# Attention and a two-product SiLU network on one core: the products' instructions rank 100 places earlier in the scheduler

## The chip, the cores and the metric

The kernel runs on one core of one Trainium2 chip. The metric is the device time of one execution in microseconds (us); several runs are taken and their median is given. A core has TensorE (PE; its weight loads are listed apart as PEld), VectorE (DVE), ScalarE (ACT), GpSimd (POOL) and SyncE (SP), which here only issues DMAs. Each engine works through its own list of instructions in order and waits on semaphores for the others.

## The reference

Attention with a second, linear memory read, over 8 batches and 8 heads of 576 tokens and 64 features, all in float32; then a network without bias on the 4608 x 512 result. The inputs q, k, v, M_prev, z_prev and beta belong to the first part, the two weights to the second (they arrive as 64-bit floats).

```python
scores = scale * np.matmul(q, k.transpose(0, 1, 3, 2))
scores = np.where(causal, -1000000000.0, scores)
a = np.exp(scores - scores.max(-1, keepdims=True))
a /= a.sum(-1, keepdims=True) + 1e-09
local = np.matmul(a, v)
q_p = phi(q)                                   # where(x > 0, x, exp(x) - 1) + 1
mem_out = einsum('bhsd,bhde->bhse', q_p, M_prev) / (einsum('bhsd,bhd->bhs', q_p, z_prev)[..., None] + 1e-06)
attn = g * mem_out + (1 - g) * local           # g = sigmoid(beta), one per head
x = attn.transpose(0, 2, 1, 3).reshape(B * S, H * D)
h = x @ w_in                                   # 4608 x 512 by 512 x 2048
out = (h * (1.0 / (1.0 + np.exp(-h)))) @ w_out # 4608 x 2048 by 2048 x 512
```

## The kernel before

**Two streams and a third.** Attention (`attention`, with `scores` and `values` for each head) goes over the 64 heads, the eight heads of a batch in a row. The products (`ffn`) go over 18 units of 256 tokens. A unit can begin when all eight heads of the last batch that it touches are done: units 0 and 1 need 8 heads, 2 and 3 need 16, 4 and 5 need 24, 6 to 8 need 32, 9 and 10 need 40, 11 and 12 need 48, 13 and 14 need 56, the rest 64. The third stream (`preparation`) turns the 32 pieces of the weights into a high and a low float32r part; twelve of the pieces are written to a scratch in memory and streamed from there again for each unit (`flow`), the others stay in place.

**A head.** `scores` transposes q and k on DVE (line 221), splits them into a high and a low part (lines 230 to 237; the first ten heads are left whole and multiplied in float32), makes four score tiles and two halves of the fifth (matmuls of lines 250, 271 and 274), each with a masked minimum on DVE (252, 284) and an exponential on ACT (254, 294), scales them on POOL (304) and works out the memory read's features (lines 325 to 334). `values` transposes features and probabilities on TensorE (351, 376, 384, 393), copies them out in two parts (lines 358, 359, 406, 407), multiplies them by M_prev and v (414, 422) and writes half a head at a time into the tile `xt` of its two heads (line 430, for the first ten heads line 425).

**A unit.** `split_x` copies and splits the tokens (lines 504 and 505: four tiles `xu` out of six buffers). Then come eight steps p: 24 matmuls of 256 columns into `h` (line 552), which has one PSUM bank, and every second time one of two others once all heads are traced; the 12 matmuls of 512 columns of the step before into the two accumulators `acc` (line 532); then tanh on ACT (563), the product with h on DVE (564, which gives the bank of h free), and the two parts of `g` on POOL (567) and DVE (568). At p = 6 the next unit's split is traced if its heads are done. At the end `acc` goes out (578).

**What sets the order.** The streams are Python generators. The loop at line 589 takes one step of attention at a time, some preparation, and as many steps of the products as the rates 0.20 (first two units) and 0.22 (later) allow: 17 steps make a unit, and ten steps of attention a head. What is left of the products when attention's generator ends is traced after the loop. The order of tracing is an instruction's place. It isn't yet the order of the engines' lists: the tile framework simulates the program in time and gives each engine, whenever it comes free, the instruction with the lowest place among those whose data and buffers are there. So an engine may take work from far later in the program if nothing earlier is ready. SP's list of DMAs, on which all loads stand (attention's two heads ahead, the streamed weights when one of two buffers comes free), is made in the same way.

Of the kernel before, what the change touches and what calls it, by code (L numbers as in the profile page):

```python
# [33 lines left out]
FFN_RATE = 0.22  # L34
FIRST_RATE = 0.2
FIRST_UNITS = 2
W_EARLY = 2


@with_exitstack  # L40
def memory_attention_then_silu_ffn(ctx, tc, q, k, v, M_prev, z_prev, beta, w_in, w_out, out):
# [132 lines left out]
    def load_next(n):  # L174
        if n < len(order):
            with tc.issue_after(anchor["sp"]) if "sp" in anchor else ExitStack():
                loaded.append(load_weight(*order[n]))

    def preparation():
        for n, x in enumerate(order):  # L180
            with tc.issue_after(anchor["dve"]):
                split_weight(*x, loaded.pop(0))
            load_next(n + W_AHEAD)
            ready.add(x)
            yield
# [13 lines left out]
    def load_rest(b, h):  # L199
        qn = qrest[(b * H + h) % 2]  # L200
        nc.sync.dma_start(out=qn[:, 0:NQ - 1], in_=q[b, h, 0:(NQ - 1) * P].rearrange("(c p) d -> p c d", p=P))
        nc.sync.dma_start(out=qn[0:LAST, NQ - 1], in_=q[b, h, S - LAST:S])
        vr = pool.tile([P, NQ, D], F32, tag="vr", name="vr", bufs=3)
        nc.sync.dma_start(out=vr[:, 0:NQ - 1], in_=v[b, h, 0:(NQ - 1) * P].rearrange("(c p) d -> p c d", p=P))
        for p0 in (0, LAST):
            nc.sync.dma_start(out=vr[p0:p0 + LAST, NQ - 1], in_=v[b, h, (NQ - 1) * P:S])
        mr = pool.tile([P, D], F32, tag="mr", name="mr", bufs=NB["mr"])
        for p0 in (0, 64):
            nc.sync.dma_start(out=mr[p0:p0 + 64], in_=M_prev[b, h])
        zb = pool.tile([P, D], F32, tag="zb", name="zb", bufs=NB["zb"])  # L210
        anchor["sp"] = nc.sync.dma_start(out=zb, in_=z_prev[b, h:h + 1].to_broadcast([P, D])).ins
        return qn, vr, mr, zb
# [223 lines left out]
    def attention():  # L436
        todo = [(b, h) for b in range(B) for h in range(H)]
        raws, rests = [], []
        for n in range(2):
            raws.append(load_raw(*todo[n]))  # L440
            if n == 0:
                load_next(0)
            rests.append(load_rest(*todo[n]))
            if n == 0 and W_EARLY > 1:
                load_next(1)
        for n in range(W_EARLY, W_AHEAD):
            load_next(n)
        second = iter(())
        for n in range(len(todo) + 1):

            first, made = iter(()), {}
            if n < len(todo):
                first = scores(*todo[n], raws.pop(0), rests.pop(0), made, n < N_WHOLE)
            one = two = True
            m = 0
            while one or two:
                for _ in range(FIRST_STEPS):
                    one = one and next(first, "end") != "end"
                if two and next(second, "end") == "end":
                    two = False  # L460
                    done[0] = n
                if m == 2 and n + 2 < len(todo):
                    raws.append(load_raw(*todo[n + 2]))
                m += 1
                yield
            if n < len(todo):
                b, h = todo[n]
                if n + 2 < len(todo):
                    rests.append(load_rest(*todo[n + 2]))
                if h % 2 == 0:  # L470
                    xt[b, h // 2] = pool.tile([P, S], F32, tag=f"xt{h // 2}", name="xt", bufs=2)
                second = values(b, h, made, xt[b, h // 2], n < N_WHOLE)
# [113 lines left out]
    att, prep, prod = attention(), preparation(), ffn()  # L586
    steps, produced, steps_made = 0, 0.0, 0
    going = True
    while going:
        going = next(att, "end") != "end"  # L590
        steps += 1
        started = done[0] >= H
        while going and len(ready) < min(2 * KF, steps * (PREP_AFTER if started else PREP_RATE) / A_STEPS):
            next(prep)
        if started:
            produced += (FFN_RATE if steps_made >= FIRST_UNITS * F_STEPS else FIRST_RATE) * F_STEPS / A_STEPS
        while going and produced >= 1.0:
            said = next(prod, "end")
            if said == "wait":
                produced = min(produced, 1.0)  # L600
                break
            if said == "prepare":
                next(prep)
                continue
            produced -= 1.0
            steps_made += 1
# [28 lines left out]
```

## Time and profile before

| what | value |
|---|---|
| median of 3 runs | 1333.85 us (1330.49 to 1334.98) |
| the profiled execution: its own time | 1331.87 us |
| its span, first to last instruction | 1330.1 us |
| mean granted TensorE clock | 0.978 |
| TensorE busy: matmuls, weight loads | 1269.9 us (95%), 1084.7 us (82%) |
| DVE, ACT, POOL busy | 963.4, 805.2, 798.1 us |
| DMA | 190.39 MB, 143 GB/s, 50.8% of 16 engines' span |

A row of the page or of a view by line names the line of the kernel, the engine, the operation, and what is written from what by the program's names. Rows in order of time begin with the start and the duration in us, and show in brackets how long the engine sat idle before and who ended that. Rows by stretch give the stretch, its length, and then the busy time of each engine with the number of instructions; behind them stand the granted clock, the DMA engines' share and GB/s. The ends of matmuls are modelled, so neighbouring matmuls overlap in the rows.

### The profile page before, as it was taken

The numbers are of one execution on the slowest core, as the hardware profiler recorded it, in microseconds if no ns is written. First come the engines' busy times: TensorE is split into PE (matmuls) and PEld (weight loads), VectorE is DVE, ScalarE is ACT, GpSimd is POOL, SyncE is SP. The second block draws the span as 40 slices with busy tenths as digits, with TensorE's granted clock in tenths as the row PEclk, the third lists the DMA queues.
The fourth block names the chain that finished last, engine by engine and source line by source line (L and its number), as shares of the span: only waits on it lengthen the run. The fifth ranks groups of instructions, "written<-read, shape, count | busy, mean of one in ns | idle before, by whom it ended". The sixth has DMA issues, their size and how long they took to land.

```text
span 1330.1 us, 24649 instructions
## 1 busy us (share of the span) xinstructions
PE 1269.9 (95%) x7858; PEld 1084.7 (82%) x7858; DVE 963.4 (72%) x2580; ACT 805.2 (61%) x1999; POOL 798.1 (60%) x1169
## 2 busy tenths in 40 slices
PE   6988989999999999999999999999999999999998
PEld 2343458898989899899989898989898889899997
DVE  7988985788888878877888787778878875322222
ACT  6777765667676767667776676666767663111111
POOL 6888994676666667766677665656576653101110
PEclk9986799999999999999999999999999999999999
DMA  6766555554555545555555455455545432444444
GB/s 163 191 177 176 151 152 159 136 140 134 135 150 137 151 116 135 152 137 151 136 149 140 136 139 136 131 149 136 137 134 145 128 101 80 155 137 155 156 159 143
DMA packets 302994, 190.39 MB, mean 143 GB/s; under 512 B 258832, under 2 KB 267024, under 8 KB 302864
## 3 DMA queue, kind: packets, MB, share of 16 engines
q1 hardware_dynamic: 302864, 188.82, 50.8%
q8 instruction: 62, 1.02, 0.3%
q14 instruction: 68, 0.56, 0.1%
HBM read 173.02 MB, written 15.73 MB: 142 GB/s over the span
## 4 chain that ended last, share of the span: by engine, by line
PE 71%; DVE 13%; ACT 6%; DMA 4%; issue 3%; POOL 2%; SPq 1%; DVEq 0%; POOLq 0%; ACTq 0%
PE h L552 27%; PE acc L532 24%; PE x L422 7%; PE s L250 5%; PE tp L376 4%; DVE s L252 2%; PE x L414 1%; PE tq L351 1%; DMA zb<-in_z_prev 1%; DVE xu L505 1%; DMA flow<-wo_s 1%; DVE th L564 1%; DVE wy L152 1%; DVE wy L159 1%; ACT p L254 1%
## 5 line engine op out<-in xcount | busy, mean ns | idle before, releaser
L552 PE MATMUL h<-xu,wi 128*128 128x256 f32 x2592 | 373.8, 287 | 10.0 <-DVE th L564 7.3
L552 PEld LDWEIGHTS h<-xu,wi 128*128 128x128 f32 x2592 | 342.6, 191 | 24.9 <-DVE th L564 5.9
L304 POOL TENSOR_SCALAR p<-p,st 128x384 f32<-128x384 f32 (+3 forms) x320 | 186.1, 600 | 127.4 <-DVE st L302 121.2
L532 PE MATMUL acc<-wo,g 128*128 128x512 f32 x864 | 244.8, 399 | 0.0
L567 POOL TENSOR_SCALAR g<-th 128x512 fp32r<-128x512 f32 x144 | 90.9, 631 | 236.8 <-DVE th L564 205.7
L532 PE MATMUL acc<-flow,g 128*128 128x512 f32 x864 | 230.9, 395 | 0.7 <-DMA flow<-wo_s 0.7
L254 ACT ACTIVATE p<-s,st 128x128 f32<-128x128 f32 (+3 forms) x256 | 134.9, 528 | 123.2 <-DVE st L252 93.7
L564 DVE SCALAR_TENSOR_TENSOR th<-th,h 128x512 f32<-128x512 f32 x144 | 98.5, 685 | 130.5 <-ACT th L563 128.0
L532 PEld LDWEIGHTS acc<-flow,g 128*128 128x128 f32 x864 | 158.9, 188 | 33.9 <-DMA flow<-wo_s 1.8
L532 PEld LDWEIGHTS acc<-wo,g 128*128 128x128 f32 x864 | 150.0, 189 | 20.1 <-POOL p L304 0.5
L563 ACT ACTIVATE th<-h 128x512 f32<-128x512 f32 x144 | 85.6, 595 | 128.1 <-PE h L552 127.3
L407 DVE TENSOR_TENSOR pl<-tp,ph 128x384 fp32r<-128x384 f32 x216 | 118.4, 550 | 38.1 <-ACT ph L406 33.9
L568 DVE TENSOR_TENSOR g<-th,g 128x512 fp32r<-128x512 f32 x144 | 104.8, 728 | 50.5 <-POOL g L567 49.3
L252 DVE CUSTOM_DVE_ANT_0 s<-s,mask 128x128 f32<-128x128 f32 (+3 forms) x256 | 125.4, 492 | 11.5 <-PE s L250 6.7
L376 PE MATMUL tp<-ident,p 128*128 128x128 f32 x640 | 123.0, 292 | 8.5 <-DVE qp L359 3.7
L552 PE MATMUL h<-xu,flow 128*128 128x256 f32 x864 | 126.7, 284 | 0.0
L406 ACT CAST ph<-tp 128x384 fp32r<-128x384 f32 x216 | 104.7, 490 | 23.6 <-PE x L422 14.7
L552 PEld LDWEIGHTS h<-xu,flow 128*128 128x128 f32 x864 | 114.1, 190 | 0.9 <-issue 0.3
L376 PEld LDWEIGHTS tp<-ident,p 128*128 128x128 f32 x640 | 81.5, 147 | 37.4 <-POOL p L304 9.3
L235 POOL TENSOR_TENSOR ql<-tt,qq 64x512 fp32r<-64x512 f32 x54 | 73.2, 1356 | 20.6 <-ACT qq L231 11.3
L328 POOL TENSOR_TENSOR r<-e,zb 128x320 f32<-128x320 f32 x64 | 59.8, 935 | 42.4 <-DVE e L327 35.4
L422 PE MATMUL x<-pl,vs 128*128 128x256 f32 x324 | 81.7, 307 | 0.0
(103 smaller groups left out, 2430.2 us busy)
## 6 DMA issues: line engine op xcount, KB each, us to landing
flow<-wo_s SPq DMA_DIRECT2D x144, 512.0 KB, 3.5
flow<-wi_s SPq DMA_DIRECT2D x72, 512.0 KB, 3.8
raw<-in_k SPq DMA_DIRECT2D x128, 72.0 KB, 2.3
raw<-in_q SPq DMA_DIRECT2D x128, 72.0 KB, 2.5
out<-o SPq DMA_DIRECT2D x36, 256.0 KB, 4.2
wraw<-in_moe_w_in SPq DMA_DIRECT2D x16, 512.0 KB, 4.4
qn<-in_q SPq DMA_DIRECT2D x64, 128.0 KB, 2.9
vr<-in_v SPq DMA_DIRECT2D x64, 128.0 KB, 2.6
```

Source lines behind the costliest of these rows:

```text
L252: anchor["dve"] = nc.vector.tensor_tensor_reduce(s, s, mask[:, 3 * P - P * i:], QS, 3.0e38, ALU.add, ALU.min, st[:, i:i + 1]).ins
L254: nc.scalar.activation(pt, s, AF.Exp, bias=st[:, i:i + 1], scale=-1.0, accum_out=st[:, 10 + i:11 + i])
L304: nc.gpsimd.tensor_scalar(pb[x], pb[x], st[:, 15 + x:16 + x], 1.0, op0=ALU.mult, op1=ALU.mult)
L376: nc.tensor.transpose(t[:, o:o + P], pb[i][:, P * j:P * j + P], ident)
L406: nc.scalar.copy(ph[:, 0:o], t[:, 0:o])
L407: nc.vector.tensor_tensor(out=pl[:, 0:cut], in0=t[:, 0:cut], in1=f(ph[:, 0:cut]), op=ALU.subtract)
L422: nc.tensor.matmul(x[0:rows, q0:n], vs[0:n_k, j], part[0:n_k, o:o + n - q0], start=False, stop=last)
L532: nc.tensor.matmul(acc[t], ta, tb, start=p == 0 and c == 0 and n == 0, stop=p == NP - 1 and c == 1 and n == len(terms) - 1)
L552: nc.tensor.matmul(h[:, c], ta, tb, start=kk == 0 and n == 0, stop=kk == KD - 1 and n == len(terms) - 1)
L564: nc.vector.scalar_tensor_tensor(out=th, in0=th, scalar=1.0, in1=h, op0=ALU.add, op1=ALU.mult)
L567: nc.gpsimd.tensor_scalar(hi, th, 1.0, 1.0, op0=ALU.mult, op1=ALU.mult)
L568: nc.vector.tensor_tensor(out=lo, in0=th, in1=f(hi), op=ALU.subtract)
```

## The change

The call that advances the products' generator by one step is put into a context that sets the place counter back by 100 for the instructions traced in it and restores it on leaving. Matmuls, vector work, the splits and the loads of streamed weights that are traced inside the loop all get these places. The products' steps traced after the loop, preparation and attention keep theirs. Nothing is computed in another way.

```diff
+AHEAD = 100
 ...
         while going and produced >= 1.0:
-            said = next(prod, "end")
+            with tc.high_priority(AHEAD):
+                said = next(prod, "end")
             if said == "wait":
                 produced = min(produced, 1.0)
                 break
```

## The prediction

> **What bounds the kernel now.** I read the page's shares and slices first, then the busy time by stretch, then the waits, then the order of time at the places where a unit of the products begins.
>
> ```profile
> PE 1269.9 (95%) x7858; PEld 1084.7 (82%) x7858; DVE 963.4 (72%) x2580; ACT 805.2 (61%) x1999; POOL 798.1 (60%) x1169
> PE   6988989999999999999999999999999999999998
> PEclk9986799999999999999999999999999999999999
> ...
> 0.00:180.00 180.00, 148.99 (x428) 67.39 (x428) 152.88 (x359) 132.92 (x316) 151.51 (x156) 0.86 0.63 168
> 180.00:1050.00 870.00, 848.42 (x5667) 769.62 (x5667) 698.61 (x1977) 595.41 (x1506) 582.95 (x909) 1.00 0.52 140
> 1050.00:1331.00 281.00, 272.47 (x1766) 247.70 (x1764) 111.89 (x246) 76.83 (x178) 63.65 (x106) 1.00 0.41 135
> ```
>
> The first rows are the page; the last three give length and then busy PE, PEld, DVE, ACT and POOL in a stretch. TensorE is the bound. Of its 60 us of idle time, 31.0 lie before 180 us (180 - 148.99), where attention runs without the products: the first unit of 256 tokens needs all heads of the first batch, so the change has nothing to put there. From 180 to 1050 us, where both run, 21.6 us are idle (870 - 848.42). That is the most that a better order can win there. The last stretch has 8.5 (281 - 272.47), drain at the end included.
>
> ```profile
> 250.00:1050.00 800.00, 779.90 (x5243) 713.14 (x5241) 649.06 (x1845) 553.28 (x1396) 538.18 (x845) 1.00 0.51 139
> ...
> 250.00:1050.00 800.00, 319.72 (x2218) 290.39 (x2218) 1.00 0.51 139
> 1140.00:1320.00 180.00, 100.70 (x765) 99.30 (x766) 1.00 0.46 153
> ...
> 250.00:1050.00 800.00, 42.39 (x94) 1.00 0.51 139
> ```
>
> All engines; then line 552's matmuls in the shared stretch and in the tail; then line 430's DVE additions, two a head. A unit has 192 matmuls of line 552. In the tail, where nothing else runs, 765 of them in 180 us are 3.98 units, **45.2 us of TensorE a unit**. In the shared stretch 2218 are 11.55 units and 94 halves are 47 heads: 17.0 us a head, 4.07 heads a unit. Of 779.9 us, 11.55 x 45.2 = 522 are the products', so a head takes (779.9 - 522) / 47 = **5.5 us of TensorE**. The rest of a head's 17.0 us is the products' filling.
>
> **The change, part by part.** No instruction is added or removed. The scheduler gives each engine, in simulated time, the ready instruction with the lowest place. Entering the context sets the place back by 100 and leaving restores it, so products traced in the loop rank 100 places earlier against attention. Those traced after the loop are not moved.
>
> How much is 100 places? One late head traces 41 matmuls and transposes, 27 DVE, 20 ACT and 16 POOL instructions and 12 DMAs (counted in the code): 116, so 0.86 head. If the releases of its some 40 tiles take places too, 0.64. I take 0.75 head. A unit's 17 steps at 0.22 x 17 / 9 a step are traced over 4.09 heads, so a head's place of products is 45.2 / 4.09 = 11.05 us of TensorE. TensorE is full, so what the products gain attention loses: x / 11.05 + x / 5.5 = 0.75 gives x = 2.75 us. The products come 2.75 us sooner; attention falls behind by 2.75 / 5.5 = 0.5 head, 8.5 us. **The shift between them is 11.3 us** (12.9 at 0.86, 9.6 at 0.64).
>
> *What is saved: waits of the h buffer.* It has one bank until attention is over.
>
> ```profile
> PE h L552 <- DVE th L564: 4.6, 8, 1.2
> PE h L552 <- DVE th L564: 7.3, 11, 1.6
> ...
> 797.13 0.28 PE L250 MATMUL s<-kk,ql 128*128 128x256 f32 x1
> 798.60 2.77 PE L552 MATMUL h<-xu,wi 128*128 128x256 f32 x21 [1.19 <-DVE th L564]
> ...
> 796.15 0.42 DVE L505 TENSOR_TENSOR xu<-xt,xu 128x256 fp32r<-128x256 f32 x1
> 796.49 0.82 DVE L290 TENSOR_TENSOR st<-st 64x1 f32<-64x1 f32 x1
> 797.24 0.41 DVE L505 TENSOR_TENSOR xu<-xt,xu 128x256 fp32r<-128x256 f32 x1
> 797.68 0.15 DVE L291 COPY st<-st 64x1 f32<-64x1 f32 x1
> 797.86 0.69 DVE L564 SCALAR_TENSOR_TENSOR th<-th,h 128x512 f32<-128x512 f32 x1
> ```
>
> The wait rows (total us, times, longest) are of 250 to 1050 us and of the whole span; below them stands one of these waits, with DVE's order ahead of it. Attention's L290 and L291 stand before th there (0.82 + 0.15 us) and would stand behind it. I take -4.6 us, between 0 (the splits, themselves products, delay th too) and -7.3.
>
> In a sentence by itself: the Trainium skill, Perfetto Trace Analysis, Optimization Strategy, says that a gap which repeats on the engine that should be full can mean too few buffers for the next tile. The eight waits fit it, since one bank is released late each time; by that rule a new order would leave them, and the sum below would be 4.6 us higher.
>
> *What is lost: tokens not yet there.* Units 2, 4 and 6 are the first to read a new batch, and their last split waits for that batch's eighth head.
>
> ```profile
> 314.64 0.49 DVE L505 TENSOR_TENSOR xu<-xt,xu 128x64 fp32r<-128x64 f32 x2
> 323.18 1.54 PE L532 MATMUL acc<-flow,g 128*128 128x512 f32 x6
> ...
> 450.70 0.42 DVE L430 TENSOR_TENSOR xt<-x,xb 64x256 f32<-64x256 f32 x1
> 453.20 1.04 DVE L505 TENSOR_TENSOR xu<-xt,xu 128x256 fp32r<-128x256 f32 x2
> 456.36 1.54 PE L532 MATMUL acc<-flow,g 128*128 128x512 f32 x6
> ...
> 589.88 1.33 DVE L505 TENSOR_TENSOR xu<-xt,xu 128x192 fp32r<-128x192 f32 x5 [1.62 <-ACT xu L504]
> 597.43 1.55 PE L532 MATMUL acc<-flow,g 128*128 128x512 f32 x6
> ...
> 0.00:318.90 318.90, 7.80 (x20) 0.92 0.59 158
> 0.00:318.90 318.90, 4.97 (x11) 0.92 0.59 158
> 0.00:798.60 798.60, 30.33 (x67) 0.97 0.55 148
> ```
>
> At each of the three: the splits end, and the last matmuls of the unit before end (which keep TensorE supplied). The slack is 324.7 - 315.1 = 9.6 us, 457.9 - 454.2 = 3.7, and 599.0 - 591.2 = 7.8; at unit 4 the head itself is only written at 451.1. The last rows count half heads written by lines 425 (20, the first ten heads) and 430: 31 are done when unit 2 begins, 87 when unit 9 begins at 798.6, which needs 80. From unit 9 on over three heads are in hand, so no later unit binds. A shift of 11.3 leaves the products without tokens for 1.7 + 7.6 + 3.5 = 12.8 us. Then TensorE has attention alone, at a pace between 17.0 us a head and what DVE allows:
>
> ```profile
> 250.00:1050.00 800.00, 129.48 (x184) 55.31 (x93) 57.64 (x92) 1.00 0.51 139
> 250.00:1050.00 800.00, 319.72 (x2218) 290.39 (x2218) 26.99 (x60) 17.63 (x60) 1.00 0.51 139
> ```
>
> (DVE, ACT, POOL of tile th; PE, PEld, DVE, ACT of tile xu.) Attention's DVE time is (649.06 - 129.48 - 26.99) / 47 = 10.5 us a head. So TensorE is 32% (5.5 / 17.0) to 52% (5.5 / 10.5) used while blocked; at the middle, 42%, it idles 58% of 12.8 us: **+7.4 us**. Ends: 0 if attention is not pushed back at all; at 0.86 head 3.3 + 9.2 + 5.1 = 17.6 us x 0.68 = +12.0.
>
> *The clock.* A gap costs more than itself:
>
> ```profile
> 463.86 0.67 PE L250 MATMUL s<-kk,qq 128*128 128x384 f32 x1 [2.32 <-ACT p L254]
> 868.86 0.52 PE L376 MATMUL tp<-ident,p 128*128 128x128 f32 x3 [2.87 <-DVE qp L359]
> 463.90:467.30 3.40, 3.40 (x13) 3.10 (x14) 3.27 (x11) 2.68 (x7) 1.94 (x4) 0.50 0.95 207
> 870.10:873.50 3.40, 3.40 (x18) 3.40 (x18) 3.28 (x11) 1.30 (x5) 0.78 (x2) 0.50 0.49 86
> ```
>
> After the two gaps of over 2 us the granted clock is 0.50 for 3.4 us: 1.7 us lost each. I count one more: +1.7, with ends 0 and +5.1 (three). The Trainium skill, TensorE: Matmul & The Clock Gate, What's actually happening, puts the drop after an idle window of about 3.4 us; here 2.3 and 2.9 us sufficed, so the trace is the stricter, and by the page's figure this term would be 0.
>
> *Priced at nothing.*
>
> ```profile
> POOL p L304 <- DMA raw<-in_q: 5.8, 2, 5.2
> L162 POOL TENSOR_TENSOR flow<-wy,flow x12: 1262/1380/1723, 39.6 to 195.5; 128x512 fp32r<-128x512 f32 x12
> 1133.10 0.49 DVE L430 TENSOR_TENSOR xt<-x,xb 64x320 f32<-64x320 f32 x1 [3.25 <-ACT xb L429]
> ```
>
> The 12 loads of streamed weights a unit on SP's queue now pass attention's loads. These are issued two heads ahead, 34 us, against a delay of under 10; without that cover a late load costs what the largest such wait shows, 5.2 us. The products' ACT, DVE and POOL work comes first: an attention instruction waits one more of 0.3 to 0.8 us, and DVE is 81% busy (649 / 800), so TensorE's filling covers it; without cover it is the blocked time already counted. In the tail attention ends some 8 us later, at 1142 instead of 1134 us, over four units (180 us) of waiting products: only the order changes. The weights' preparation ends at 197 us (its last POOL subtraction) and isn't moved; only the first unit of the products could meet it.
>
> **The sum.** -4.6 + 7.4 + 1.7 = +4.5 us on the profiled execution's 1331.87 (span 1330.1 and 1.8 around it): 1336.4. The median of the runs stands 2.0 above that execution, which would give 1338.4; I say 1337. A measurement of this kernel can tell about 0.3%, 4 us.
>
> **The rivals.**
>
> *Attention isn't pushed back (faster).* What follows the scores of a head lies about two heads behind the products' place (unit 2's first matmul, traced late in head 17, runs when 15 heads are done), so most of attention keeps its rank even against a place 100 earlier. Then nothing blocks, the h waits go, and a third of the other 17 us of idle time (21.6 - 4.6) goes with them, as TensorE gets products sooner after each gap: -4.6 - 5.7, 1322 to 1324 with the runs' offset. Against it: scores and products run neck and neck in places, and scores must precede what follows.
>
> *The tokens bind fully (slower).* Place: the starts of units 2, 4 and 6. At 0.86 head and 32% use of TensorE, with the h waits left and three clock drops: +12.0 + 5.1 = +17.1, 1349 to 1351. It decides from a shift of about 10 us on, where the lost time passes the saved. For it: the slack at unit 4 is 3.7 us. Against it: attention, once alone, should speed up.
>
> *The h waits stay, the rest as forecast.* The splits and one bank delay th, not attention: 1336.4 + 4.6 = 1341. For it: splits stand ahead of th in the rows above. Against it: so do L290 and L291. It is the mechanism of the page on repeated gaps named above.
>
> *The lists hardly change.* TensorE was full and the products already ran at the edge of their tokens, so 100 places move little: 1334.
>
> **How the numbers follow.** The forecast has 0.36 (own range 1331 to 1343, its terms' nearer ends), not pushed back 0.30, tokens bind 0.14, h waits stay 0.12, hardly changed 0.08. Faster by over 0.3% (below 1329.9) takes the second and 0.05 of the first, 0.35; slower (above 1337.9) takes 0.14, 0.10 of the h case and 0.11 of the forecast, 0.35; the rest, 0.30, is within. The range reaches to both outer cases: 1321 to 1351.
>
> **What would show it.** Right: line 552's waits for th nearly gone from 250 to 1050 us; idle TensorE at the starts of units 2, 4 and 6 with waits for the splits (L505), longest at unit 4; granted clock 0.50 after them; the last head done some 8 us later, and the tail at 45 us a unit as before. Wrong: heads done at the same times as now (attention not pushed back), or new TensorE waits for exponentials (ACT p L254) all through, which would mean that attention's own chain, not the tokens, became late.

## The result: 1.3% slower, no more than lists differ by edits that prefer nothing

The changed kernel takes 1348.39 us (median of 4 runs, 1347.56 to 1356.03) against 1333.61 us before (median of 4): a ratio of 1.0128, 95% interval 1.0097 to 1.0159. Its profiled execution takes 1349.06 us, 17.2 more than that of before. Everything of the kernel shifts down by one line, so line 552 of before is 553 here.

The page of the changed kernel, shares and slices, then its busy time by stretch (length, then PE, PEld, DVE, ACT, POOL):

```profile
PE 1284.0 (95%) x7858; PEld 1088.8 (81%) x7858; DVE 959.4 (71%) x2580; ACT 803.0 (60%) x1999; POOL 806.5 (60%) x1169
PE   6988999999989899999999998999999999999998
PEclk9977799999999999999999999999999999999999
...
0.00:180.00 180.00, 153.76 (x427) 68.28 (x428) 151.72 (x359) 132.89 (x316) 152.32 (x156) 0.82 0.63 168
180.00:1050.00 870.00, 840.08 (x5555) 757.18 (x5554) 683.25 (x1933) 581.73 (x1476) 577.49 (x889) 0.99 0.52 138
1050.00:1348.00 298.00, 290.14 (x1880) 263.35 (x1878) 124.48 (x290) 88.39 (x209) 76.66 (x126) 1.00 0.42 135
```

TensorE's busy time rose by 14 us with the same 7858 matmuls, so the busy share can't say what was lost. The count of matmuls can: the first 180 us hold 427 against 428, the stretch from 180 to 1050 us holds 5555 against 5667. At 5667 in 870 us, 6.5 a us, these 112 are 17 us. The whole loss lies there. Idle time explains 8.3 us of it (29.9 against 21.6, that is 870 less the busy time). The clock explains about 5:

```profile
318.20:321.60 3.40, 1.55 (x10) 1.12 (x8) 3.18 (x13) 2.35 (x8) 1.64 (x4) 1.00 0.52 113
321.60:325.00 3.40, 2.88 (x13) 2.91 (x14) 2.73 (x8) 2.50 (x7) 3.40 (x7) 0.51 0.60 107
464.90:468.30 3.40, 2.45 (x11) 1.27 (x11) 1.95 (x7) 3.01 (x7) 3.34 (x7) 1.00 0.70 119
468.30:475.10 6.80, 5.35 (x25) 5.19 (x25) 5.02 (x12) 3.85 (x10) 5.50 (x7) 0.51 0.48 157
823.30:826.70 3.40, 3.40 (x19) 3.40 (x18) 2.82 (x10) 0.00 (x0) 0.37 (x2) 0.52 0.57 104
895.00:898.40 3.40, 3.40 (x15) 3.06 (x14) 3.27 (x12) 1.80 (x7) 2.29 (x5) 0.51 0.54 96
```

These are stretches of the changed kernel; the column behind POOL is the granted clock. In all some 17 us ran at half clock against 6.8 before, so 8.5 us lost against 3.4. What is left is some 4 us. It may be pauses that the modelled ends of the matmuls hide; that isn't shown.

Who made TensorE wait (total us, times, longest), from 250 to 1050 us, before:

```profile
PE h L552 <- DVE th L564: 4.6, 8, 1.2
PE tp L376 <- DVE qp L359: 3.7, 2, 2.9
PE s L250 <- ACT p L254: 3.6, 4, 2.3
PE x L422 <- ACT ph L406: 1.1, 2, 0.5
```

and in the changed kernel:

```profile
PE s L251 <- ACT p L255: 6.9, 10, 2.8
PE h L553 <- DVE th L565: 4.7, 6, 1.7
PE x L423 <- ACT ph L407: 2.8, 4, 1.4
PE x L423 <- POOL vs L317: 2.4, 2, 1.7
PE h L553 <- DVE st L303: 2.4, 1, 2.4
```

The products' waits for th are as long as before. Attention's scores and products with v now wait twice as long for ACT, and for POOL's vs, which did not hold TensorE in these rows before. Over all rows of the stretch the waits named at attention's matmuls rise from 14.2 to 20.3 us and those at the products' from 5.3 to 7.4: together about the 8.3 us of idle time. No matmul waits for a DMA there with the change (0.2 us before).

### The profile page after: what moved, and what is told of

The parts are those of the page before. It is cut to its first block, busy times and chain, and to the rows that moved or that the text cites. A ratio compares the mean times of both kernels' runs of the same rounds, so it can differ in the third digit from the quotient of the medians.

```text
span 1347.2 us, 24644 instructions
## 1 busy us (share of the span) xinstructions
PE 1284.0 (95%) x7858; PEld 1088.8 (81%) x7858; DVE 959.4 (71%) x2580; ACT 803.0 (60%) x1999; POOL 806.5 (60%) x1169
## 5 line engine op out<-in xcount | busy, mean ns | idle before, releaser
L553 PE MATMUL h<-xu,wi 128*128 128x256 f32 x2592 | 385.8, 289 | 8.4 <-DVE th L565 5.6
L553 PEld LDWEIGHTS h<-xu,wi 128*128 128x128 f32 x2592 | 348.4, 192 | 23.1 <-issue 8.6
L305 POOL TENSOR_SCALAR p<-p,st 128x384 f32<-128x384 f32 (+3 forms) x320 | 193.1, 622 | 101.5 <-DVE st L303 101.1
L533 PE MATMUL acc<-wo,g 128*128 128x512 f32 x864 | 248.2, 398 | 0.2 <-DVE g L569 0.2
L533 PE MATMUL acc<-flow,g 128*128 128x512 f32 x864 | 239.5, 398 | 0.6 <-DMA flow<-wo_s 0.4
L569 DVE TENSOR_TENSOR g<-th,g 128x512 fp32r<-128x512 f32 x144 | 110.5, 768 | 55.7 <-POOL g L568 54.7
L377 PE MATMUL tp<-ident,p 128*128 128x128 f32 x640 | 126.3, 291 | 7.9 <-POOL p L305 4.7
L553 PE MATMUL h<-xu,flow 128*128 128x256 f32 x864 | 130.7, 287 | 0.0
L236 POOL TENSOR_TENSOR ql<-tt,qq 64x512 fp32r<-64x512 f32 x54 | 72.9, 1349 | 36.3 <-issue 18.5
L423 PE MATMUL x<-ph,vs 128*128 128x320 f32 (+4 forms) x378 | 79.7, 278 | 6.4 <-POOL vs L317 3.6
```

Of the source, the lines that this page charges most:

```text
L305: nc.gpsimd.tensor_scalar(pb[x], pb[x], st[:, 15 + x:16 + x], 1.0, op0=ALU.mult, op1=ALU.mult)
L377: nc.tensor.transpose(t[:, o:o + P], pb[i][:, P * j:P * j + P], ident)
L423: nc.tensor.matmul(x[0:rows, q0:n], vs[0:n_k, j], part[0:n_k, o:o + n - q0], start=False, stop=last)
L533: nc.tensor.matmul(acc[t], ta, tb, start=p == 0 and c == 0 and n == 0, stop=p == NP - 1 and c == 1 and n == len(terms) - 1)
L553: nc.tensor.matmul(h[:, c], ta, tb, start=kk == 0 and n == 0, stop=kk == KD - 1 and n == len(terms) - 1)
L569: nc.vector.tensor_tensor(out=lo, in0=th, in1=f(hi), op=ALU.subtract)
```

## Experiments

Two theories of the shift came first. **Tokens bind**: the products reach units 2, 4 and 6 before the tokens do. **Attention late throughout**: products stand ahead of attention on every engine, attention's operands come late, and TensorE, which takes its list in order, stops at them. Each ratio below is to runs of the kernel before that were timed beside the run.

**The context in one half only.** With LATE = 7 units as the border:

```diff
-            with tc.high_priority(AHEAD):
+            with tc.high_priority(AHEAD) if steps_made >= LATE * F_STEPS else ExitStack():
```

> The context only from the eighth unit on (units 0 to 6 keep their places), so it acts only where tokens are far ahead. Tokens bind at units 2, 4 and 6 (the forecast's rival): nothing is left of the loss, 1328 to 1335 us. Attention's instructions come late all through, and TensorE, which works in order, stops at them: some six of thirteen moved units still pay, 1339 to 1343 us.

Measured: 1334.02 us, ratio 0.9998 (0.9977 to 1.0019). With `<` in place of `>=`:

> The context only up to the seventh unit. Tokens bind: the whole loss, 1346 to 1350 us. Attention late all through: its share, 1340 to 1344 us. The two kernels' losses should add up to that of the change (14.8 us) in either case.

Measured: 1354.38 us, ratio 1.0144 (1.0116 to 1.0172), above both ranges. By themselves the two speak for the tokens: all of the loss in units 0 to 6, nothing later. The rows by stretch speak against it. The changed kernel lacks 73 matmuls from 180 to 660 us, about where its seventh unit ends (the next begins at 670), and 40 more from 660 to 1050. The kernel with the context in the early half lacks 75 and then 71. Here are the later stretches, before and with the early half:

```profile
660.00:1050.00 390.00, 377.80 (x2540) 345.19 (x2538) 315.87 (x890) 265.16 (x671) 257.00 (x406) 1.00 0.51 138
660.00:1050.00 390.00, 374.30 (x2469) 340.38 (x2468) 304.40 (x871) 260.76 (x663) 258.39 (x399) 0.98 0.50 135
```

So the early kernel loses nearly as much behind the border, where no place is set back any more, as ahead of it.

**0 and -100 places.** Only the constant differs.

```diff
-AHEAD = 100
+AHEAD = 0
```

> The context with 0 instead of 100: on leaving it the counter is restored, so the products' instructions share places with the attention that follows instead of taking their own, but nothing is set back. Either theory of the shift: as before, 1331 to 1337 us. If it is the restoring, not the 100 places, that costs: 1345 us or more.

Measured: 1351.93 us, ratio 1.0120 (1.0099 to 1.0140). No instruction is set back, and the loss is as large, as that text foresaw if the restoring is what costs. With -100:

> The context with -100: the products rank 100 places later. Attention late through rank: attention's operands come earlier, TensorE stops less at them, 1325 to 1333 us. Tokens bind only: more slack than needed at the three units, nothing won elsewhere, 1331 to 1336 us. If products behind attention starve TensorE's filling (h waits grow beyond the 7.3 us of before): 1338 us or more.

Measured: 1344.98 us, ratio 1.0063 (1.0042 to 1.0084): no gain, though attention did come earlier at first (the 16th head is done at 312.6 us against 321.5; the last one at 1140.1 against 1133.6). The text's third case, longer waits for h, did occur: 10.4 us against the 7.3 of before. But 3 us are not 9, and at 0 places the waits are as long (10.8). Preferring the products, preferring attention and only sharing places all cost time. That fits neither theory and raised a third: the lists of before are a **lucky draw**, and whatever makes the scheduler's simulation run otherwise draws others. A draw here means one set of lists.

**Disturbing the lists without any preference.** The kernel before, with three added memsets:

```diff
-    nc.gpsimd.memset(pair, BIG)
+    for _ in range(4):
+        nc.gpsimd.memset(pair, BIG)
```

> The kernel before with a memset at the start done four times instead of once (three more of 0.42 us on GpSimd, before the heads). No place moves against another, but the scheduler's simulation starts otherwise and its lists part from the sixth matmul on. If the loss comes from the order that the change prefers: as before, within 2 us. If the list of before is a lucky one, which any disturbance loses: 5 to 20 us more than before.

Measured: 1357.28 us, ratio **1.0154** (1.0132 to 1.0176). The added work is 3 x 0.42 us by the row of one such memset; the kernel loses some 21. Its rows by stretch:

```profile
0.00:180.00 180.00, 151.01 (x397) 64.76 (x398) 154.46 (x353) 129.98 (x310) 148.49 (x156) 0.77 0.64 170
180.00:1050.00 870.00, 841.00 (x5560) 759.67 (x5559) 688.74 (x1946) 585.57 (x1488) 573.30 (x891) 0.99 0.52 137
```

5560 matmuls in the shared stretch against 5667, as many as the change gives, and 31 fewer ahead of it; the eighth head is done 3.0 us later, at 183.3. So a disturbance that prefers nothing costs more than the change. The same memsets in the changed kernel:

> The changed kernel with the same three memsets more. If the loss belongs to the preference: as the change, 1346 to 1351 us. If each list is a draw: anywhere from 1333 to 1355 us, and not tied to the change's 1348.

Measured: 1362.80 us, ratio 1.0198 (1.0182 to 1.0214), above both ranges.

**The shift without the restoring.** The counter goes on, so the products keep taking places of their own:

```diff
-            with tc.high_priority(AHEAD):
-                said = next(prod, "end")
+            tc.cur_priority -= AHEAD
+            said = next(prod, "end")
+            tc.cur_priority += AHEAD
```

> The products set back by 100 places, but the counter goes on behind them as in the kernel before (nothing is restored), so 100 places are half a head instead of 0.88. Tokens bind: half the shift, 1336 to 1343 us. If the restoring is what costs (0 places cost as much as 100): 1332 to 1337 us. If each list is a draw: no relation to either.

Measured: 1336.63 us, ratio 1.0007 (0.9990 to 1.0023): 100 places, half a head here, cost nothing. The time lies in the range of half the shift and in that of the restoring, so it does not decide between the two.

**More draws, in pairs.** The kernel before at another rate, then two disturbances with and without the change: a memset of the set-up moved, and FIRST_RATE = 0.201.

> The kernel before with the products' rate at 0.221 instead of 0.22: the last unit in the loop comes 0.06 of a unit sooner, and the matmul list is the same up to the 1552nd. By any theory of preference: as before, within 2 us. If the list of before is a lucky one: 5 to 20 us more.

Measured: 1336.95 us, ratio 1.0016 (0.9996 to 1.0035), 1.2 us above the runs beside it: as before. The 5 to 20 us of the lucky list did not come here.

```diff
+    pair = const.tile([P, 3 * P], F32, name="pair")
+    nc.gpsimd.memset(pair, BIG)
     mask = const.tile([P, 4 * P], F32, name="mask")
 ...
-    pair = const.tile([P, 3 * P], F32, name="pair")
-    nc.gpsimd.memset(pair, BIG)
```

> The kernel before with one memset of the set-up moved ahead of two others on GpSimd: no work added, no place moved that matters; the matmul list parts at the 47th, and 6722 of 7710 matmuls stand where they stood. If a loss needs added work at the start (the three memsets) or the change's preference: 1333 to 1338 us. If each list is a draw of its own: 1333 to 1357 us, nearer to before the more of the list is kept.

Measured: 1343.51 us, ratio 1.0061 (1.0039 to 1.0084): a loss without added work.

> The changed kernel with the same memset moved; 5952 of 7710 matmuls stand where the change puts them. If the preference costs 15 us as such: 1346 to 1351 us, 12 to 18 above the run beside it without the change. If each list is a draw: a difference from that run between -5 and 25 us.

Measured: 1348.75 us, ratio 1.0103 (1.0079 to 1.0127): 5.2 us above the run beside it, not the 12 to 18 of a fixed price.

> The kernel before with the rate of the first two units at 0.201 instead of 0.2; the matmul list parts at the 601st and keeps 2116 of 7710 positions. Any theory of preference: 1332 to 1339 us, since the products' places move by less than one step. If each list is a draw: 1333 to 1357 us, a loss more likely than not if the list of before is a lucky one.

Measured: 1337.16 us, ratio 1.0020 (1.0002 to 1.0039), which both cases allow.

> The changed kernel with the same rate of 0.201. If the preference costs 15 us as such: 12 to 18 us above the run beside it without the change. If each list is a draw: a difference between -10 and 25 us.

Measured: 1354.57 us, ratio 1.0143 (1.0118 to 1.0168): 17.4 us above the run beside it, which both cases allow.

**What follows.** Ratios to the kernel before, the stretches of one stream in TensorE's list (a new one begins whenever it passes from attention to the products or back), the pauses of TensorE at matmuls, and the time at half clock. Where a cell has two numbers, the second is with the change:

| disturbance | without the change | with it | difference | stretches | pauses at attention's 250, 376, 422 | at the products' 532, 552 | half clock, 190 to 1300 us |
|---|---|---|---|---|---|---|---|
| none | 1 | 1.0128 | 0.0128 | 1004, 1120 | 38.8, 54.5 us | 42.6, 42.9 us | 6.8, 17.1 us |
| three memsets | 1.0154 | 1.0198 | 0.0044 | 1028, 1096 | 45.1, 53.3 | 46.1, 47.9 | 23.9, 17.1 |
| memset moved | 1.0061 | 1.0103 | 0.0042 | 1004, 1138 | 39.5, 48.9 | 43.1, 43.1 | 23.9, 13.7 |
| first rate 0.201 | 1.0020 | 1.0143 | 0.0123 | 1060, 1134 | 43.9, 47.3 | 40.3, 45.4 | 6.8, 23.9 |

The pauses are worked out from the starts of all matmuls after 190 us: what the distance from one start to the next exceeds the usual one of that line and shape (the 20th percentile in the kernel before), put down to the line of the second, half-clock windows left out. They are good to about 1 us.

1. Lists that differ by nothing but a disturbance lie up to 1.5% apart, more than the 1.28% in question. The kernel before lies at the fast end of its five draws: two are slower by 0.6 and 1.5%, two (the rates of 0.201 and 0.221) can hardly be told from it.
2. All four differences are positive, 0.84% or 11 us on average. From their own spread a 95% interval is 0.08% to 1.6%. But the first pair starts from the kernel that seems to be the good draw; the other three alone give 0.70% with an interval from below zero (-0.5%) to 1.8%. So the change probably costs something; its size is known only roughly.
3. On average the kernels with the change pause 9.2 us longer at attention's three matmul groups and 1.8 us longer at the products' (51.0 - 41.8 and 44.8 - 43.0), and their lists pass more often between the streams. But pair by pair the growth at attention (15.7, 8.2, 9.4, 3.4 us) does not follow the price (0.0128, 0.0044, 0.0042, 0.0123): the last pair has the least growth and nearly the highest price. It does once the products' pauses and the half clock, half of which is lost, are added: 21, 7, 4 and 17 us. So the clock seems to be a part of what a draw decides. The moved memset without the change pauses hardly longer than the kernel before (1.2 us in all); it spends 17 us more at half clock, 8.5 us lost, which is about its whole loss (7.4 us). That is a correlation over four pairs and one profile of each kernel, not a removal of the cause.
4. What in the change costs isn't settled. The shift alone costs nothing, and the restoring alone (0 places) 1.2%, but each is one draw, and draws differ by as much. The same holds for the two halves.

No version beat the kernel before.

## Why the prediction was right or wrong

The time lies in the range and on the side that had 0.35, as much as faster. The forecast of 1337 was 11 us short. The time of the rival that lets the tokens bind (1349 to 1351) nearly came out, but mostly for another reason. That the range held is in part luck: it was wide enough for gain and loss, and of the steps below only the size of the shift and the tail held.

**The shift: right in size, wrong in its parts.** By the count that the text of the shift-alone run gives, 100 places are 0.88 head, beside the 0.86 of the prediction's upper end. The eighth head's first half and unit 2's start, in the kernel before and then in the changed one:

```profile
310.74 0.43 DVE L430 TENSOR_TENSOR xt<-x,xb 64x256 f32<-64x256 f32 x1
318.90 1.30 PE L552 MATMUL h<-xu,wi 128*128 128x256 f32 x9
```

```profile
314.60 0.43 DVE L431 TENSOR_TENSOR xt<-x,xb 64x256 f32<-64x256 f32 x1
316.30 0.35 DVE L506 TENSOR_TENSOR xu<-xt,xu 128x192 fp32r<-128x192 f32 x1
309.05 1.24 PE L553 MATMUL h<-xu,wi 128*128 128x256 f32 x9
312.40 1.55 PE L533 MATMUL acc<-flow,g 128*128 128x512 f32 x6
316.25 0.28 PE L553 MATMUL h<-xu,wi 128*128 128x256 f32 x1
322.12 1.41 PE L553 MATMUL h<-xu,wi 128*128 128x256 f32 x5 [2.37 <-DVE st L303]
```

Products 9.9 us sooner, tokens 3.9 us later: a shift of 13.7 us where 12.9 stood at 0.86 head (9.6 to 12.9 in all). The text had it the other way round, the products 2.75 us sooner and attention 8.5 later.

**Tokens not there: reached at unit 2 alone, and cheap there.** The nine matmuls of 309.05 use the three splits that exist; the last products of the unit before end at 313.95, and the next can start at 316.25. So the products were without tokens for 2.3 us, where the text had 1.7. But TensorE was not idle in them: from 313.9 to 316.4 attention's matmuls keep it busy throughout, and only 0.2 us of waiting are put down to the splits. What unit 2 pays comes just after: the 2.37 us before 322.12, for which the products of the unit before are already used up, and half of the 3.4 us at half clock behind it, some 4 us in all. By unit 3 the lead is gone (its first matmul starts at 383.6 us against 384.0 before). At units 4 and 6:

```profile
453.81 0.90 DVE L506 TENSOR_TENSOR xu<-xt,xu 128x128 fp32r<-128x128 f32 x4
461.85 1.09 PE L533 MATMUL acc<-flow,g 128*128 128x512 f32 x4
...
596.16 0.48 DVE L506 TENSOR_TENSOR xu<-xt,xu 128x192 fp32r<-128x192 f32 x2
602.55 1.31 PE L533 MATMUL acc<-flow,g 128*128 128x512 f32 x5
```

The slack from the splits' end to the products' end is 8.2 and 7.2 us, not used up. The 7.6 + 3.5 us of blocking that the text put there did not come: the text used the same full shift at all three units. (Its slack of 7.8 us at unit 6 should be 8.2: the row of five splits, which ends at 591.2, includes the first of unit 7; the last of unit 6 ends at 590.8.)

**The h waits: wrong.** The term of -4.6 us measured +2.0. From 250 to 1050 us the products wait 4.7 us for th, and the 2.4 put down to L303 is th's bank too, 7.1 in all; before it was 4.6 and 0.5 put down to L290, 5.1. The step that failed is that attention's small DVE work would stand behind th. In the wait that ends at 322.12 it does not:

```profile
319.09 0.60 ACT L564 ACTIVATE th<-h 128x512 f32<-128x512 f32 x1
321.29 0.68 DVE L565 SCALAR_TENSOR_TENSOR th<-th,h 128x512 f32<-128x512 f32 x1
```

Tanh ends at 319.69; DVE then runs five of attention's instructions, and th ends only at 321.97. The rival that keeps these waits had this right. The trace agrees with the rule on repeated gaps in the Trainium skill, Perfetto Trace Analysis, Optimization Strategy, as the prediction used it: the waits for the one bank stayed under a new order. No run has a second bank, so the cure isn't shown.

**The clock: mis-sized.** +1.7 forecast, +5.1 measured in the profiled execution, which is the end of the text's range (three more drops).

**The cover priced at nothing: wrong.** This is the step that failed most. Attention's vector work was said to be covered by TensorE's filling, and its waits were put at nothing; they rose by 6.1 us. Waits of scores for exponentials, which the text named as a sign of being wrong, rose from 3.6 to 6.9 us. The filling is not there when it is needed. The longest of these waits, with the products next in the list and the th that gives their bank free:

```profile
822.28 0.44 PE L251 MATMUL s<-kk,qq 128*128 128x384 f32 x1 [2.75 <-ACT p L255]
822.76 2.37 PE L553 MATMUL h<-xu,wi 128*128 128x256 f32 x12
...
821.93 0.68 DVE L565 SCALAR_TENSOR_TENSOR th<-th,h 128x512 f32<-128x512 f32 x1
```

The bank comes free at 822.61, after attention's wait has ended. So it is nearly everywhere: of the 20.3 us of waits named at attention's matmuls from 250 to 1050 us, the next product in TensorE's list was ready in 0.9 us only (before: 0.2 of 14.2), counting a step of h as ready when th of the step before has ended. The idle time arises where both streams run dry at once, and the name of the wait shows only the one that stands first.

The tail held, though not its delay: the last head is done 18.6 us later, not 8, and the rest of the kernel behind it takes as long as before (195.0 us against 196.5).

```profile
1151.75 0.49 DVE L431 TENSOR_TENSOR xt<-x,xb 64x320 f32<-64x320 f32 x1 [3.24 <-ACT xb L430]
```

**Missing altogether: the draw.** No term and no rival said that a new list may lose 20 us for no reason of preference (the three memsets). That spread is as large as the 15 us to be explained, so how much of them the change itself costs stays open.

## What to carry to other kernels

Where a simulated scheduler makes the lists, any edit can draw new ones, and the kernel at hand may sit on a good draw: price the change, then add a spread for the draw (here 0.2 to 1.5%, all to the slow side). To learn what an edit itself does, time it under a few neutral disturbances, each with and without it, and look at the differences. Single runs of parts of the edit, however tight their intervals, don't tell them apart from the draw. And where a busy engine waits, look at what stands next in its list: the wait may be named after one stream while the other has nothing ready either.

## What the runs showed of the hardware

The clock fell to half without an idle gap as long as the 2.3 us of the kernel before: in the 3.4 us ahead of two of the changed kernel's drops TensorE was busy, in pieces, for 2.05 us (891.6 to 895.0) and even 2.45 us (464.9 to 468.3), and no idle time in them was longer than 0.8 us. So several short waits close together can be followed by 3.4 us at half clock, a further 1.7 us lost. Busy time alone doesn't tell when: from 454.8 to 458.2 TensorE was busy for 2.01 us, with an idle gap of 1.39, and the clock stayed full. From 190 to 1300 us every stretch at half clock in the kernels of the table lasted 3.4 us or twice that.
